# A store queued two heads later: the attention output's DMA behind the stack copies

## The chip, the cores and the metric

The kernel runs on one core of a Trainium2 chip. The metric is the time of one execution on the device in microseconds (us), and the kernel's time is the median over its runs. Beside the timed runs stands one profiled execution, whose trace gives the start and end of every instruction. A core has five instruction streams: TensorE (PE, with its weight loads shown as PEld), VectorE (DVE), ScalarE (ACT), GpSimd (POOL) and SyncE (SP). Here SP issues every DMA of the kernel, one after the other, in the order of its program: an instruction at the head of SP's queue that waits for data holds up all DMAs behind it.

## The reference, cut to what matters

```
x: 2048 tokens x 1024 channels, 32 heads of 32, 4 segments of 512 tokens
h = layernorm(x) * (1 + ca) + sa
q, k, v = h @ wq, h @ wk, h @ wv
for s in range(4):                                   # segments
    p = softmax(q_s k_s^T * scale + mask)            # causal, per head
    a_dot = p @ v_s
    a_mem = phi(q_s) M / (phi(q_s) z + 1e-6)
    o_s = g * a_mem + (1 - g) * a_dot                # g = sigmoid(beta), per head
    M += phi(k_s)^T v_s;  z += sum(phi(k_s))
x = x + ga * (o @ wo)
h = layernorm(x) * (1 + cb) + sb
x = x + gb * mixer(h)                                # two matrix products over the tokens, with GELU between
```

`sa`, `ca`, `ga`, `sb`, `cb`, `gb` come from `silu(c) @ w_mod`. The change touches only how `o` is carried to device memory between the attention and the product with `wo`.

## The kernel before, in words

The attention works in 32 iterations `t` (list `its`, line 313). One iteration is a group of four heads `g` and a segment `seg`: first all eight groups with segments 0 and 1, then all eight with segments 2 and 3. Within an iteration there are four heads `h`, so that there are 128 heads in all, numbered `n = 4 * t + h`. The loop at line 621 runs over `n` as a software pipeline. In step `n` it traces

- `scores` of head `n` (line 459): the product of queries and keys for the softmax, into PSUM; exponentials on ACT, the causal cut on POOL, and a split into two half-precision parts;
- `maxima` of head `n + 3` (LEADS, line 421): row maxima of that product. After each odd head the negated maxima of two heads are transposed into `nt`, and four small DMAs (line 445) put them into rows 96 and 97 of the stack tiles of the two heads, where `scores` reads them;
- `values` of head `n - 1` (VL, line 483): the product with the values. After the fourth head of an iteration four transposes put the iteration's output into PSUM (`ops`, line 510), ACT copies it to `ot` in SBUF (line 512; one buffer), and SP stores `ot` to the tensor `oT` in device memory (line 513);
- one piece of `project` for `n + 8` (LEADP, line 329): pieces 0 and 1 make keys and values, piece 2 transposes the keys, makes the queries, splits both into the tile `sg` (one buffer) and calls `stack` for heads 0 to 2, piece 3 calls `stack` for head 3;
- whatever `plan` has put down for step `n` in the table `todo`: weight prefetches, splits, stores of split weights.

`stack` (line 319) builds the operand tile `sk` of one head with three DMAs of 128 KB from `sg` (lines 325 to 327). There are eight such tiles, four for even and four for odd iterations.

So within step `4t + 4` the output of iteration `t` is finished and stored, and in step `4t + 6` the nt copies for heads 0 and 1 of iteration `t + 2` and the stacks of heads 0 to 2 of iteration `t + 3` are traced.

After the loop `out_proj` (line 688) reads `oT` in blocks of 128 tokens across all groups (`otr`, line 691) and multiplies with `wo` (line 706). Its blocks go in the order 0, 1, 8, 2, 9, and so on; blocks 0 to 7 lie in segments 0 and 1, blocks 8 to 11 in segment 2, which the last group stores in iteration 30, and 12 to 15 in segment 3, stored in iteration 31.

The order of instructions on each engine isn't the order of the text. A planner, asked for at line 997, goes through the traced instructions with a simulated timeline and puts each on its engine's queue when it is ready there; where several are ready, the one traced earlier goes first. `tc.issue_after(ins)` adds an edge: what is traced in its block on the engine of `ins` comes behind `ins` in that engine's queue. The edge orders the queue and is no wait for completion.

`marks` (line 448) holds, by head number and engine, an instruction behind which planned work may be put: V, A and G stand for DVE, ACT and POOL. The helper `behind(n, engines)` (line 451) opens such an edge for the mark of exactly that head, if there is one. The table `todo` and `plan` are defined at lines 592 to 595, and the loop takes a step's entries at line 642.

Of the kernel before, what the change touches and what calls it, by code (L numbers as in the profile page):

```python
# [7 lines left out]
F32 = mybir.dt.float32  # L8
# [9 lines left out]
S, D, H, DH, F = 2048, 1024, 32, 32, 3584  # L18
P = 128
NSEG, L = 4, 512  # L20
# [9 lines left out]
LEADP, LEADS, NSK = 8, 3, 8  # L30
XB = 4
VL = 1
# [8 lines left out]
LEADP = 8  # L41
LEADS = 3


def attention_and_mlp(ctx, tc, x, wq, wkv, wo, beta, w1, b1, w2, b2, c, wm_a, wm_b, out):
    nc = tc.nc
    V, A, G, T, SY = nc.vector, nc.scalar, nc.gpsimd, nc.tensor, nc.sync

    dram = ctx.enter_context(tc.tile_pool(name="dram", bufs=1, space=DRAM))
    oT = dram.tile([NG, P, S], F32, name="oT")  # L50
# [24 lines left out]
    def bank(tag, bufs, name):  # L75
        return psum.tile([P, 512], F32, tag=tag, bufs=bufs, name=name)
# [65 lines left out]
    def new_page(name):  # L142
        return page.tile([P, 2, 512], F32R, tag="page", bufs=16, name=name)
# [32 lines left out]
    def load_w(g, pr):  # L176
        res = W[pr, g] = {}
        for kind, part in (("v", 0), ("v", 1), ("q", 0)):
            load_part(g, pr, kind, part, res)
        if pr == 0:  # L180
            keep_w(g)
# [113 lines left out]
    b = late.__enter__()  # L295
# [12 lines left out]
    def reload_h(seg, ct):  # L308
        pg = new_page(f"h{seg}_{ct}")
        SY.dma_start(pg.bitcast(F32), hT1[seg - 2, ct])  # L310
        hpages[seg, ct] = pg
# [3 lines left out]
    st = {}  # L315

    last_sk = {}

    def stack(t, h):


        sk = st[t]["sk", h] = skt[t % 2][h]
        skf = sk.bitcast(F32)
        src = st[t]["sg"].bitcast(F32)[32 * h:32 * h + 32]
        SY.dma_start(skf[0:32], src[:, 0:3:2])
        SY.dma_start(skf[32:64], src[:, 0:4:3])
        last_sk[t, h] = SY.dma_start(skf[64:96], src[:, 1:3])

    def project(t, piece):
        pr, g, seg = its[t]  # L330
# [27 lines left out]
        elif piece == 2:  # L358
# [26 lines left out]
            for h in range(3):  # L385
                stack(t, h)
# [34 lines left out]
    def maxima(t, h):  # L421
        d = st[t]
        if h % 2 == 0:
            d["mx"] = b.tile([P, 2, 4], F32, tag="mx", bufs=2, name=f"mx{t}_{h}")
        mx = d["mx"]
        q, k = d["sk", h][0:96, 0], d["sk", h][0:96, 1]
        x = bank("s1", 2, f"sx_{t}_{h}")
        y = bank("s1", 2, f"sy_{t}_{h}")
        z = bank("s1", 2, f"sz_{t}_{h}")
        for i, o in ((0, x[:, 0:128]), (2, x[:, 128:512]), (1, y[:, 0:256]), (3, z)):  # L430
            T.matmul(o, q[:, 128 * i:128 * i + 128], k[:, 0:128 * i + 128], start=True, stop=True)  # L431
            marks[4 * t + h - LEADS, "V"] = V.tensor_tensor_reduce(  # L432
                o, o, mask[:, 384 - 128 * i:], 1.0, -3.0e38, op0=ALU.add, op1=ALU.max,
                accum_out=mx[:, h % 2, i:i + 1])
        if h % 2 == 0:
            return
        ps = bank("ms", 1, f"nmps{t}_{h}")
        T.transpose(ps[0:8, 0:128], mx.rearrange("p a b -> p (a b)"), ident)
        nt = [b.tile([8, P], F32R, tag=f"nt{i}", bufs=2, name=f"nt{i}_{t}_{h}") for i in range(2)]
        A.activation(nt[0], ps[0:8, 0:128], AF.Copy, scale=-1.0)  # L440
        V.scalar_tensor_tensor(nt[1], ps[0:8, 0:128], -1.0, nt[0].bitcast(F32), op0=ALU.mult, op1=ALU.subtract)
        for hh in range(2):
            sk = d["sk", h - 1 + hh]
            for part in range(2):
                SY.dma_start(sk[96 + part:97 + part, 0].bitcast(F32).rearrange("p (b n) -> p b n", n=128),
                             nt[part][4 * hh:4 * hh + 4].bitcast(F32))

    marks = {}

    @contextmanager  # L450
    def behind(n, engines):

        with ExitStack() as s:
            for e in engines:
                if (n, e) in marks:
                    s.enter_context(tc.issue_after(marks[n, e].ins))
            yield

    def scores(t, h):
# [23 lines left out]
    def values(t, h):  # L483
        pr, g, seg = its[t]
        d = st[t]
        am, ph = d["am"], d["ph", h]
        pv = bank("pv", 1, f"pv{t}_{h}").rearrange("p (a n) -> p a n", a=4)
        col = {0: lambda i: 128 * i, 1: lambda i: 512 + 128 * (i - 1), 2: lambda i: 1024 + 128 * (i - 2),
               3: lambda i: 896}
        n = 0  # L490
        for part, w in ((0, NV), (1, 65)):
            for i in range(4):
                for j in range(i + 1):
                    o = col[j](i)
                    T.matmul(pv[:, i, 0:w], ph[:, part, o:o + 128], d["vp"][:, j, h, 0:w], start=(n == 0),  # L495
                             stop=(n == 19), skip_group_check=True)
                    n += 1
        V.reciprocal(pv[:, :, 0], pv[:, :, 0])
        red = r_.tile([P, 4, 32], F32, tag="red", bufs=2, name=f"red{t}_{h}")
        V.tensor_reduce(red, pv[:, :, 1:97].rearrange("p a (c e) -> p a e c", c=3), axis=AX.X, op=ALU.add)  # L500
        ah = am[:, :, 32 * h:32 * h + 32]
        V.scalar_tensor_tensor(red if seg else ah, red, gate[:, 1, 4 * g + h:4 * g + h + 1],
                               pv[:, :, 0:1].to_broadcast([P, 4, 32]), op0=ALU.mult, op1=ALU.mult)
        if seg:
            G.tensor_tensor(ah, ah, red, op=ALU.add)
        if h < 3:
            return
        ps = bank("ms", 1, f"ops{t}")
        for i in range(4):
            T.transpose(ps[:, 128 * i:128 * i + 128], am[:, i], ident)  # L510
        ot = r_.tile([P, L], F32, tag="ot", bufs=1, name=f"ot{t}")
        A.copy(ot, ps)
        SY.dma_start(oT[g, :, L * seg:L * seg + L], ot)
        del st[t]

    mcol = const.tile([P, 4 * NK], F32, name="mcol")
# [6 lines left out]
    def mod_late(j, r):  # L523
        V.scalar_tensor_tensor(r, r, 1.0, scb, op0=ALU.mult, op1=ALU.mult, accum_out=mcol[:, j:j + 1])
        if j == 7:
            mod_rows(0, 8)
        if j == 31:
            V.tensor_scalar_add(mcol[:, 16:24], mcol[:, 16:24], 1.0)
            mod_rows(8, 32)

    def mod_rows(lo, hi):
        n = hi - lo
        ps = bank("ms", 1, f"mlt{lo}")
        T.transpose(ps[0:n, 0:128], mcol[:, lo:hi], ident)
        row = pj.tile([n, P], F32, tag="tmp", bufs=2, name=f"mrow{lo}")
        A.copy(row, ps[0:n, 0:128])
        SY.dma_start(modd.rearrange("a (b n) -> (a b) n", n=P)[lo:hi], row)

    def at(f, n):
        if 0 <= n < 4 * NI:  # L540
            f(n // 4, n % 4)
# [47 lines left out]
        for part, t in enumerate((hi, r)):  # L589
            SY.dma_start(wos[c2:c2 + 2, nh, :, part].rearrange("c p n -> p c n"), t)  # L590

    todo = {}

    def plan(n, f, engines=""):
        todo.setdefault(n, []).append((f, engines))

    def later(n, fetch, m, f, engines):

        got = []
        plan(n, lambda: got.append(fetch()))  # L600
        plan(m, lambda: f(got[0]), engines)
# [4 lines left out]
    for g in range(2, NG):  # L606
        n = 8 * g - 13
        plan(n, lambda g=g: W.__setitem__((0, g), {}))
        for kind, part, n0, n1 in (("v", 0, 0, 1), ("v", 1, 1, 3), ("q", 0, 2, 4)):
            later(n + n0, lambda g=g, kind=kind, part=part: fetch_part(g, kind, part),  # L610
                  n + n1, lambda r, g=g, kind=kind, part=part: split_part(g, kind, part, r), "A")
        plan(n + 4, lambda g=g: keep_w(g))
    for j in range(32):
        n = ML0 + MLS * j
        later(n, lambda j=j: mod_fetch(j), n + 2, lambda r, j=j: mod_late(j, r), "V")
    plan(WO0 - 3, lambda: spread(gaw, 0))
    for i in range(8):
        n = WO0 + WOS * i
        later(n, lambda i=i: wo_fetch(i), n + 2, lambda r, i=i: wo_split(i, r), "G")

    for n in range(-LEADS, 4 * NI + VL):
        at(scores, n)
        at(maxima, n + LEADS)
        at(values, n - VL)
        m = n + LEADP
        if 0 <= m + 4 < 4 * NI:
            t = (m + 4) // 4
            if its[t][:2] not in W:
                with tc.issue_after(last_sk[0, 3].ins):
                    load_w(its[t][1], its[t][0])  # L630
        if m >= 8:
            at(project, m)
        if 59 <= m < 67:
            seg, ct = 2 + (m - 59) // 4, 2 * ((m - 59) % 4)
            reload_h(seg, ct)
            reload_h(seg, ct + 1)
        if 4 * NI - 5 <= m < 4 * NI + 3:
            i = m - 4 * NI + 5
            for c in (2 * (i % 4), 2 * (i % 4) + 1):
                wop[c, i // 4] = new_page(f"wo{c}_{i // 4}")  # L640
                SY.dma_start(wop[c, i // 4].bitcast(F32), wos[c, i // 4])
        for f, engines in todo.pop(n, ()):
            with behind(n, engines):
                f()
    right.__exit__(None, None, None)
    for q in skp + [late, prj, paw]:
        q.__exit__(None, None, None)
# [227 lines left out]
    for u, (ph, g) in enumerate(units):  # L875
# [59 lines left out]
        t = tp.tile([P, 3, 512], F32, tag="tu", bufs=1, name=f"tu{g}")  # L935
# [65 lines left out]
```

## Time and profile before

| quantity | value |
|---|---|
| median of 3 runs | 2308.41 us |
| lowest and highest | 2302.83 and 2309.76 us |
| the profiled execution's own time | 2305.58 us |
| its span, first to last instruction | 2303.9 us |
| granted TensorE clock, mean | 0.983 of full |
| stores of `ot` (line 513) | 32, from 151.6 to 1075.0 us |
| stack copies, nt copies | 384 and 256 |

How rows of the profile are read. A row of a timeline has the start in us, the duration in us, the engine, the line of the kernel, the operation, output tile `<-` input tiles and a count; in brackets the idle time of the engine before it and what ended it. SPq is SP's queue of DMAs, and the duration there is that of issuing. A row of waits has who waited, for whom, the total in us, the number of times and the longest. A row of the chain of waits has start, duration and what the chain went through; "DMA" there is from issue to landing. In the rows by stretch, each engine has its busy time and, in brackets, its instructions.

### The profile page before, as it was taken

The page shows a single profiled execution, that of the slowest core. Times are in us where ns is not written, and L with a number is a line of the kernel's source. Part 1 is how long each engine was busy: PE and PEld are TensorE (multiplying, and loading weights), DVE is VectorE, ACT ScalarE, POOL GpSimd, SP SyncE. Part 2 cuts the span into 40 slices and gives each one's busy share as a digit, 9 for nine tenths or more (in the row PEclk, how much of TensorE's full clock was granted, in tenths as well). Part 3 has the DMA queues.
Part 4 walks back from the last instruction along what each step waited for, and adds up shares of the span by engine and source line. Part 5 has one row for each costly group of instructions (what it writes and reads, how often), then busy time and mean ns, then how long its engine had stood idle before and what let it go on. Part 6 is the DMA issues. An engine that isn't in the chain of part 4 may idle for free.

```text
span 2303.9 us, 38456 instructions
## 1 busy us (share of the span) xinstructions
PE 2232.7 (97%) x13866; PEld 1918.9 (83%) x13866; DVE 1703.9 (74%) x3814; ACT 1105.6 (48%) x2018; POOL 727.9 (32%) x835
## 2 busy tenths in 40 slices
PE   8989999998999999999999999999999999999999
PEld 7879888898998889977787888888887888888877
DVE  5666666775777777657988665688889787878787
ACT  5477766755656656654324333543334242424232
POOL 3165655655666767653001000023333000000000
PEclk9989999999999999989999999999999999999999
DMA  6656555677566566663466664556557441414133
GB/s 256 199 164 183 173 162 162 195 247 225 156 199 206 166 189 187 202 212 112 137 205 213 249 237 181 202 222 239 206 201 263 171 151 55 151 55 142 55 119 146
DMA packets 172593, 414.67 MB, mean 180 GB/s; under 512 B 17236, under 2 KB 71540, under 8 KB 163444
## 3 DMA queue, kind: packets, MB, share of 16 engines
q1 hardware_dynamic: 172404, 412.22, 54.7%
q8 instruction: 110, 1.80, 0.3%
q14 instruction: 79, 0.65, 0.1%
HBM read 236.23 MB, written 125.06 MB: 157 GB/s over the span
## 4 chain that ended last, share of the span: by engine, by line
PE 81%; DVE 9%; DMA 5%; ACT 2%; issue 1%; POOL 1%; SPq 0%; DVEq 0%; ACTq 0%
PE mx L798 41%; PE nps L193 14%; PE qps L201 7%; PE po L706 6%; PE pv L495 3%; DMA wr<-in_w_dram 1%; PE a L466 1%; PE sx L431 1%; DVE ac L805 1%; PE sz L431 1%; DVE bU L123 1%; PE rd L403 1%; DVE sp L123 1%; DMA sk<-nt 1%; PE a L469 1%
## 5 line engine op out<-in xcount | busy, mean ns | idle before, releaser
L798 PE MATMUL mx<-bU,sp 128*128 128x512 f32 x2352 | 537.0, 390 | 4.7 <-DVE ac L805 2.0
L798 PEld LDWEIGHTS mx<-bU,sp 128*128 128x128 f32 x2352 | 440.4, 188 | 100.8 <-DVE sp L123 2.7
L193 PE MATMUL nps<-wv,h 128*128 128x256 f32 x3072 | 438.2, 284 | 0.7 <-DVE sg L123 0.5
L798 PE MATMUL mx<-bA,sp 128*128 128x512 f32 x1764 | 432.0, 390 | 2.5 <-DVE sp L123 2.2
L120 ACT CAST sp<-wr 128x384 fp32r<-128x384 f32 (+2 forms) x408 | 217.1, 545 | 449.9 <-PE mx L798 379.6
L481 POOL TENSOR_TENSOR ph<-p,ph 128x640 f16<-128x640 f32 x256 | 379.6, 1504 | 159.0 <-ACT ph L479 153.5
L193 PEld LDWEIGHTS nps<-wv,h 128*128 128x128 f32 x3072 | 403.8, 190 | 6.8 <-DVE sg L123 0.7
L798 PEld LDWEIGHTS mx<-bA,sp 128*128 128x128 f32 x1764 | 330.5, 188 | 73.5 <-DVE sp L123 2.9
L123 DVE TENSOR_TENSOR sp<-wr,sp 128x384 fp32r<-128x384 f32 (+2 forms) x408 | 256.8, 641 | 29.4 <-ACT sp L120 29.2
L805 DVE TENSOR_TENSOR ac<-mx,ac 128x512 f32<-128x512 f32 x280 | 189.3, 685 | 91.2 <-PE mx L798 90.5
L201 PE MATMUL qps<-h,wq 128*128 128x512 f32 x768 | 200.7, 406 | 1.4 <-DVE r L356 1.4
L432 DVE CUSTOM_DVE_ANT_0 sx<-sx,mask 128x128 f32<-128x128 f32 (+1 forms) x256 | 109.5, 428 | 113.6 <-PE sx L431 111.9
L706 PE MATMUL po<-wo,ots 128*128 128x512 f32 x768 | 184.8, 400 | 5.3 <-DVE x L709 3.1
L479 ACT CAST ph<-p 128x1280 f16<-128x1280 f32 x128 | 160.8, 1257 | 41.1 <-POOL p L477 40.3
L706 PEld LDWEIGHTS po<-wo,ots 128*128 128x128 f32 x768 | 148.3, 194 | 38.0 <-issue 3.9
L201 PEld LDWEIGHTS qps<-h,wq 128*128 128x128 f32 x768 | 144.4, 194 | 30.2 <-DVE r L356 1.2
L798 PE MATMUL mx<-bB,sp 128*128 128x512 f32 x588 | 164.3, 389 | 0.0
L477 POOL TENSOR_SCALAR_AFFINE_SELECT p<-p 128x256 f32<-128x256 f32 x256 | 120.5, 480 | 129.2 <-ACT p L470 63.4
L495 PE MATMUL pv<-vp,ph 128*128 128x97 bf16 (+1 forms) x2560 | 146.6, 204 | 5.5 <-DVE mv L134 2.7
L495 PEld LDWEIGHTS <-ph 128*128 128x128 f16 x2560 | 117.5, 100 | 29.4 <-issue 12.1
L805 DVE TENSOR_TENSOR cc<-mx,cc 128x512 f32<-128x512 f32 x140 | 94.6, 683 | 49.9 <-PE mx L798 45.4
L798 PEld LDWEIGHTS mx<-bB,sp 128*128 128x128 f32 x588 | 110.4, 188 | 23.4 <-ACT bB L120 0.6
(173 smaller groups left out, 3206.0 us busy)
## 6 DMA issues: line engine op xcount, KB each, us to landing
sk<-sg SPq DMA_DIRECT2D x384, 128.0 KB
wr<-in_w_dram SPq DMA_DIRECT2D x28, 1024.0 KB
wr<-in_w_dram SPq DMA_DIRECT2D x32, 768.0 KB
bstu<-ucd SPq DMA_DIRECT2D x28, 768.0 KB
wsp<-wv SPq DMA_DIRECT2D x32, 512.0 KB
rawm<-in_wm_b_dram SPq DMA_DIRECT2D x32, 512.0 KB
wv<-wsp SPq DMA_DIRECT2D x32, 512.0 KB
pcd<-cc SPq DMA_DIRECT2D x14, 1024.0 KB
```

Source lines behind the costliest of these rows:

```text
L120: A.copy(hi, src)
L123: lo_eng.tensor_tensor(lo, src, hi.bitcast(F32), op=ALU.subtract)
L193: T.matmul(ps[:, aa], h[:, j, 128 * tt:128 * tt + 128], wt[:, i, o:o + 256], start=(n == 0), stop=(n >= 6 * NK - 2), skip_group_check=True)
L201: T.matmul(ps, wt[:, i, o:o + 128], h[:, j], start=(k + n == 0), stop=(3 * k + n == 3 * NK - 1))
L432: marks[4 * t + h - LEADS, "V"] = V.tensor_tensor_reduce(o, o, mask[:, 384 - 128 * i:], 1.0, -3.0e38, op0=ALU.add, op1=ALU.max, accum_out= ...
L477: G.affine_select(w, w, pattern=[[0, 2], [1, 128]], compare_op=ALU.is_ge, fill=0.0, base=0, channel_multiplier=-1)
L479: marks[n, "A"] = A.copy(ph[:, 0], p32)
L481: marks[n, "G"] = G.tensor_tensor(ph[:, 1, c], p32[:, c], ph[:, 0, c], op=ALU.subtract)
L495: T.matmul(pv[:, i, 0:w], ph[:, part, o:o + 128], d["vp"][:, j, h, 0:w], start=(n == 0), stop=(n == 19), skip_group_check=True)
L706: T.matmul(ps, os_[:, i, P * ct:P * ct + P], wop[ct, nh][:, j], start=(n == 0), stop=(n == 3 * NK - 1))
L798: T.matmul(ps, ops[q][:, i, P * k:P * k + P], b[:, j], start=(m == 0 and first), stop=(m == 3 * nk - 1), skip_group_check=True)
L805: V.tensor_tensor(d, ps, d, op=ALU.add)
```

## The change

The store of `ot` is no longer issued where `ot` has been copied, in step `4t + 4`. It is put down with `plan` for step `4t + 3 + VL + 2 = 4t + 6` with the engine letter "S", a new one for SP's queue.

The mark for "S" is set in two places: at the last copy of every stack, under the step in which that stack is traced (`max(h, 2)`, since heads 0 to 2 share a step), and at every nt copy. A later mark replaces an earlier one of the same step. In step `4t + 6` the nt copies come first and the stacks of iteration `t + 3` second, so that the mark is the last copy of its third stack; the store gets an edge behind that. `behind` now takes the newest mark among step `n` and the three before it. `marks` and `plan` are defined earlier in the text, and what is left in `todo` after the loop is traced there without an edge: the store of iteration 31, planned for step 130, since the loop ends with 128.

```diff
     last_sk = {}
+    marks = {}
...
-        last_sk[t, h] = SY.dma_start(skf[64:96], src[:, 1:3])
+        last_sk[t, h] = marks[4 * t + max(h, 2) - LEADP, "S"] = SY.dma_start(skf[64:96], src[:, 1:3])
...
-                SY.dma_start(sk[96 + part:97 + part, 0].bitcast(F32).rearrange("p (b n) -> p b n", n=128),
-                             nt[part][4 * hh:4 * hh + 4].bitcast(F32))
-
-    marks = {}
+                marks[4 * t + h - LEADS, "S"] = SY.dma_start(
+                    sk[96 + part:97 + part, 0].bitcast(F32).rearrange("p (b n) -> p b n", n=128),
+                    nt[part][4 * hh:4 * hh + 4].bitcast(F32))
...
-                if (n, e) in marks:
-                    s.enter_context(tc.issue_after(marks[n, e].ins))
+                m = next((i for i in range(n, n - 4, -1) if (i, e) in marks), None)
+                if m is not None:
+                    s.enter_context(tc.issue_after(marks[m, e].ins))
...
-        SY.dma_start(oT[g, :, L * seg:L * seg + L], ot)
+        plan(4 * t + 3 + VL + 2, lambda: SY.dma_start(oT[g, :, L * seg:L * seg + L], ot), "S")
...
+    for n in sorted(todo):
+        for f, _ in todo[n]:
+            f()
     right.__exit__(None, None, None)
```

`todo` and `plan` themselves are unchanged and only stand further up.

More of the change, by code (lines that the diff above doesn't have):

```diff
@@ L537, in mod_rows, with plan @@
         SY.dma_start(modd.rearrange("a (b n) -> (a b) n", n=P)[lo:hi], row)
+    todo = {}
+    def plan(n, f, engines=""):
+        todo.setdefault(n, []).append((f, engines))
     def at(f, n):
@@ L590, in wo_split @@
             SY.dma_start(wos[c2:c2 + 2, nh, :, part].rearrange("c p n -> p c n"), t)
-    todo = {}
-    def plan(n, f, engines=""):
-        todo.setdefault(n, []).append((f, engines))
     def later(n, fetch, m, f, engines):
```

## The prediction

> **What bounds the kernel now.** I read the page first, then busy time by stretch, then the waits of SP and of PE, then SP's own timeline around the stores, and last the end of the chain.
>
> The page:
>
> ```profile
> span 2303.9 us, 38456 instructions
> ...
> PE 2232.7 (97%) x13866; PEld 1918.9 (83%) x13866; DVE 1703.9 (74%) x3814; ACT 1105.6 (48%) x2018; POOL 727.9 (32%) x835
> ...
> PE 81%; DVE 9%; DMA 5%; ACT 2%; issue 1%; POOL 1%; SPq 0%; DVEq 0%; ACTq 0%
> ```
>
> TensorE sets the time: 97% of the span, 81% of the chain that ends last. A moved DMA can only be worth what TensorE waits because of DMAs. The stretches (columns: busy time of PE, PEld, DVE, ACT and POOL, granted clock, DMA share, GB/s) bound that for the attention, the only stage in which the store runs, and give the DMA load in two places used below:
>
> ```profile
> 100.00:990.00 890.00, 857.30 (x7463) 780.79 (x7463) 612.62 (x1861) 577.84 (x1059) 554.00 (x659) 0.97 0.63 184
> ...
> 516.00:526.00 10.00, 8.15 (x53) 6.96 (x52) 5.47 (x12) 5.01 (x8) 7.51 (x7) 0.88 0.90 313
> 776.00:788.00 12.00, 9.17 (x87) 8.38 (x86) 5.79 (x23) 5.42 (x12) 7.07 (x10) 0.93 0.70 199
> ```
>
> From 100 to 990 us PE is idle for 890.0 - 857.3 = 32.7 us in all, for every reason together. Next the two waits that name the argument: how long SP's queue stood at the store, and what TensorE waited for (100 to 1080 us):
>
> ```profile
> SPq L513 <- ACT ot L512: 98.5, 21, 12.7
> ```
>
> ```profile
> PE a L466 <- DMA sk<-nt: 8.2, 4, 2.8
> PE kps L363 <- DVE r L356: 7.4, 4, 4.1
> PE sz L431 <- DVE mx L432: 4.7, 5, 2.3
> ...
> PE sx L431 <- DMA sk<-sg: 1.5, 1, 1.5
> ```
>
> So the store blocks SP for 98.5 us in 21 places, which looks like much; but TensorE waits only 8.2 us (4 times) for the small copies of the negated maxima, and 1.5 us (once) for the stack copies. 9.7 us, 0.42% of the span, is all that SP's lateness shows on PE. The other rows are waits for DVE, which the store does not touch.
>
> **Was anything needed held behind the store?** The longest stall after the first ones, on SP and, beside it, on ACT:
>
> ```profile
> 841.65 2.62 SPq L445 DMA_DIRECT2D sk<-nt  x4
> 855.16 0.33 SPq L513 DMA_DIRECT2D oT<-ot  x1
> 855.59 0.37 SPq L520 DMA_DIRECT2D rawm<-in_wm_b_dram  x1
> 856.56 0.70 SPq L325 DMA_DIRECT2D sk<-sg  x1
> ...
> 866.20 0.59 SPq L327 DMA_DIRECT2D sk<-sg  x1
> ```
>
> ```profile
> 854.55 0.59 ACT L512 COPY ot<-ops 128x512 f32<-128x512 f32 x1 [3.19 <-PE ops L510]
> ...
> 855.95 0.59 ACT L120 CAST sg<-qps 128x512 fp32r<-128x512 f32 x1 [0.32 <-PE qps L201]
> ...
> 857.52 0.26 ACT L440 ACTIVATE nt<-nmps 8x128 fp32r<-8x128 f32 x1
> ```
>
> SP stands from 844.3 to 855.2 us at the store. What comes behind it is a prefetch (L520, used two heads later) and then the stack copies; but their source sg is written on ACT at 855.95, after ot, so the first stack copy starts 0.02 us after its data. The nt behind them is written at 857.52. The queue was blocked while nothing urgent was ready. I made the same comparison at all 32 stores: a stack or nt copy was ready ahead of the store and issued after it in only three places, near 333 us and 497 us, where TensorE waited for neither, and this one:
>
> ```profile
> 528.25 0.32 SPq L513 DMA_DIRECT2D oT<-ot  x1
> 529.55 0.33 SPq L520 DMA_DIRECT2D rawm<-in_wm_b_dram  x1
> ...
> 533.37 0.69 SPq L325 DMA_DIRECT2D sk<-sg  x1
> 535.45 0.65 SPq L326 DMA_DIRECT2D sk<-sg  x1
> 536.76 3.72 SPq L445 DMA_DIRECT2D sk<-nt  x4
> ```
>
> ```profile
> 544.69 0.50 PE L466 MATMUL a<-sk 98*128 98x512 f32 x1 [1.32 <-DMA sk<-nt]
> ```
>
> Here SP issues one DMA per 1.3 us, the store takes one of these slots, and TensorE then waits 1.32 us for nt. This is the one place where the old position costs TensorE anything.
>
> **The change part by part.**
>
> *Removed: the store at its old place.* Gain: one slot of 529.55 - 528.25 = 1.30 us at 528 us; elsewhere 0, covered because the data of what follows is later than ot. Bounds: 0 (TensorE's wait is filled by another DMA) to -8.2 us (all nt waits vanish). I take -1.3, since the other three nt waits have no store ahead of them.
>
> *Added: the store behind the third stack's last copy.* At 855 that is behind 866.20, 11 us later, where it waits for nothing: ot has long been written. SP issues the same number of DMAs; the store takes 0.33 us (tile view below). But there it joins a burst of twelve stack copies, and nt copies often follow. TensorE waited for nt right behind such a burst twice:
>
> ```profile
> 512.57 0.59 SPq L327 DMA_DIRECT2D sk<-sg  x1
> ...
> 517.61 2.63 SPq L445 DMA_DIRECT2D sk<-nt  x4
> ```
>
> ```profile
> 523.32 0.56 PE L466 MATMUL a<-sk 98*128 98x512 f32 x1 [1.85 <-DMA sk<-nt]
> ```
>
> ```profile
> 778.90 0.59 SPq L327 DMA_DIRECT2D sk<-sg  x1
> ...
> 781.22 2.63 SPq L445 DMA_DIRECT2D sk<-nt  x4
> ```
>
> ```profile
> 786.41 0.77 PE L466 MATMUL a<-sk 98*128 98x512 f32 x1 [2.83 <-DMA sk<-nt]
> ```
>
> A store ahead of these nt copies delays them by its issue, 0.33 us, plus its share of the transfer queues. Its size and the bounds of its landing:
>
> ```profile
> oT<-ot SPq DMA_DIRECT2D x32, 256.0 KB
> ```
>
> ```profile
> 1048.61 0.60 ACT ot L512
> ...
> 1049.23 2.34 DMA oT<-ot
> ...
> 1051.58 4.33 DMA otr<-oT
> ...
> 1057.04 9.84 PE po L706 x30
> ```
>
> Lower bound 0.33 us (bytes pass beside the copies), upper 0.33 + 2.34 = 2.67 us (nt lands only after the store). Between them I take its bytes at the rate that the queues moved in that stretch: 262 KB / 313 GB/s = 0.84 us, so 0.33 + 0.84 = 1.17 us; the stretch is at 0.90 DMA share, so nearer to shared bandwidth than to idle. Two places: +2.3 us (bounds +0.7 to +5.3).
>
> [...] Nothing measured here yet shows a small copy behind a store.
>
> *What the later store makes late.* ot has one buffer, so the next copy to ot waits for the store's landing:
>
> ```profile
> L513 SPq DMA_DIRECT2D oT<-ot x32: 319/326/1452, 151.6 to 1075.0; - x32
> ```
>
> (1075.0 - 151.6) / 31 = 29.8 us per group, 7.45 us per head. The store moves by about two heads, 15 us, and about as much is left before the next ot; the tightest is the group stored at 528 us, with its third stack and its next copy to ot here:
>
> ```profile
> 547.06 2.00 SPq L327 DMA_DIRECT2D sk<-sg  x1
> ```
>
> ```profile
> 556.25 0.59 ACT L512 COPY ot<-ops 128x512 f32<-128x512 f32 x1
> ```
>
> From 549.06 to the copy are 7.2 us, against 2.34 for landing. Covered; with that cover gone ACT would stand, at worst, some 2 us per group. The last stores have no stack behind which to go: group 29 goes behind an nt copy of its step, group 30 behind an nt copy two heads earlier, group 31 after the loop without a mark. In SP's queue nothing lies between their old and new steps, so they stay where they are: 0 us. This matters since group 30's store is on the chain: it lands at 1051.57, the load of oT waits for it, and PE goes on at 1057.04.
>
> *Other edits.* The search of up to three heads back in the helper changes no older use, since each of those finds its own head's mark: 0. Moving the plan's definition costs 0.
>
> *Sum:* -1.3 + 2.3 = +1.0 us. The profiled execution took 2305.58 us with its span of 2303.9; so 2306.6 for such an execution. The runs' median is 2308.41, 2.8 above it, and the runs lie between 2302.83 and 2309.76; I set the forecast on the median: 2309.4, called 2309.5.
>
> **The rivals.**
>
> *Slower, nt behind the store's bytes.* Place: nt copies issued within 5 us behind the third stack, where TensorE's margin is under 5 us; I count four of the nine such groups (near 451, 518, 552, 781 us). Price: 4 x 2.67 = 10.7 us, 2319. It decides from the point at which a store's landing holds nt for more than some 2 us. For: 0.90 DMA share at 516 to 526. Against: 0.70 at 776. [...]
>
> *Faster, another order.* The build orders every engine's instructions by a simulated timeline, so a moved DMA can shift copies, and with them PE's order, all through the attention. PE's 32.7 us idle is the stock: a third of it less, with the nt waits (8.2) among it, is 11 us: 2298. For: many waits are under 2 us and hang on the order. Against: neither TensorE's work nor its buffers change; the same reshuffle can lose as much.
>
> *Slower, the end.* If group 30's store is really issued two heads later, 14.9 us, the load of oT and PE's next output projection follow: 2308.4 + 14.9 = 2323. Against: no copy stands between.
>
> *The change doesn't do what it says.* If the mark isn't found, the store stays in the queue where ot is ready: 2308.4. Against: each group up to 28 has a third stack in that very step.
>
> **How the numbers follow.** Forecast 0.48; mark without effect 0.06; faster order 0.20; nt behind the store 0.21; late end 0.05. A measurement of this kernel can tell about 0.3%, 6.9 us, from no change. So same 0.54, faster 0.20, slower 0.26. The likeliest case's own range is 2302 to 2315 (0 to +8 us of unknown costs on runs that spread by 3 us either way). For 8 in 10 it is widened to 2297 (the other order and the runs' spread) and 2321 (the nt rival).
>
> **What would show it.** Right: SP's wait for ot at the store, 98.5 us, falls below 10; the store comes right behind a third stack's last copy; TensorE's wait for nt stays between 5 and 14 us; PE idle from 100 to 990 near 33 us. The nt rival: TensorE's nt wait above 15 us, with a store just ahead. Another order: PE idle moves by 8 us or more in rows that name DVE or ACT. The end: the last two stores further behind their ot copies than now. The forecast is wrong if the time moves by more than 0.3% either way.

## The result, and the profile after

| | before | after |
|---|---|---|
| median of 10 runs each | 2305.68 us | 2312.99 us |
| lowest and highest | 2300.37 and 2310.79 us | 2307.56 and 2315.30 us |
| ratio, with its 95% interval | | 1.0026 (1.0015 to 1.0037) |
| span of the profiled execution | 2303.9 us | 2311.9 us |

The forecast was 2309.5 us with no change beyond 0.3% as the likeliest case. The changed kernel is 0.26% slower: 0.0026 x 2305.68 = 6.0 us (3.5 to 8.5). (The ratio on record is not the quotient of the two medians, which is 1.0032; the ratios below aren't either.) That lies within the 0.3%, but its interval excludes "no change", and it is six times the +1.0 us of the prediction's sum. So the case that was named came, and the sum behind it was too small.

The page of the changed kernel:

```profile
span 2311.9 us, 38437 instructions
...
PE 2233.2 (97%) x13866; PEld 1922.2 (83%) x13866; DVE 1704.8 (74%) x3814; ACT 1108.6 (48%) x2018; POOL 729.0 (32%) x835
...
PE 77%; DVE 8%; DMA 8%; ACT 3%; issue 2%; POOL 2%; SPq 1%; DVEq 0%; ACTq 0%; POOLq 0%
```

TensorE's busy time is the same (2232.7 us before, 2233.2 after). Of the 8.0 us of span 7.5 are idle time of TensorE, and in the chain that ends last the DMAs' share rises from 5% to 8%. By stretch, first after and then before (columns: busy time of PE, PEld, DVE, ACT and POOL, granted clock, DMA share, GB/s):

```profile
100.00:990.00 890.00, 853.86 (x7395) 777.97 (x7394) 610.49 (x1854) 578.06 (x1054) 550.17 (x652) 0.97 0.62 184
990.00:1080.00 90.00, 78.99 (x560) 64.00 (x559) 56.66 (x159) 47.38 (x76) 53.39 (x63) 0.87 0.54 171
```

```profile
990.00:1080.00 90.00, 82.22 (x525) 66.74 (x524) 61.95 (x159) 45.25 (x73) 46.97 (x54) 0.87 0.55 182
```

In the attention PE is idle for 890.0 - 853.86 = 36.1 us against 32.7 before, and in the 90 us around the attention's end for 11.0 us against 7.8. The two make 6.7 of the 8.0 us. This sets one execution against one other; e9 below shows how far two of the same order differ.

SP's wait at the store, and TensorE's waits from 100 to 1080 us, both after:

```profile
SPq L514 <- ACT ot L513: 11.2, 2, 9.7
```

```profile
PE a L467 <- DMA sk<-nt: 6.8, 6, 3.0
PE sx L432 <- DMA sk<-sg: 6.0, 3, 4.1
PE sx L432 <- DVE mx L433: 6.0, 9, 1.4
PE sy L432 <- DVE mx L433: 4.9, 7, 2.2
PE pv L496 <- DVE red L503: 4.7, 3, 1.9
```

The stall of SP fell from 98.5 us in 21 places to 11.2 in 2, and TensorE got nothing for it. SP stands elsewhere instead: its wait for ACT to write nt grew from 42.3 to 68.3 us. TensorE's nt wait fell only from 8.2 to 6.8 us, and the wait for stack copies rose from 1.5 to 6.0. Added up by what was waited for, over all rows from 100 to 1080 us, the waits for DMAs went from 9.7 to 12.8 us, for DVE from 22.9 to 25.7, for POOL from 1.3 to 3.6. The store stands where the change puts it, here inside the burst, with nt 5 us behind it, and TensorE waits for that nt 3.03 us (1.85 before):

```profile
512.50 0.59 SPq L328 DMA_DIRECT2D sk<-sg  x1
513.14 0.58 SPq L514 DMA_DIRECT2D oT<-ot  x1
513.82 0.61 SPq L326 DMA_DIRECT2D sk<-sg  x1
...
518.45 2.63 SPq L446 DMA_DIRECT2D sk<-nt  x4
```

```profile
414.79 0.45 PE L432 MATMUL sx<-sk 96*128 96x128 f32 x1 [4.14 <-DMA sk<-sg]
...
522.56 0.56 PE L467 MATMUL a<-sk 98*128 98x512 f32 x1 [3.03 <-DMA sk<-nt]
```

The move also changed the planner's order. The instruction lists of the two kernels differ on PE in 6186 of 13610 positions, on DVE in 1043 of 3262, and among SP's other DMAs in 361 of 1206. Two theories follow. PLACE: the store costs by standing among the stack copies, ahead of nt. ORDER: the place is harmless, and the other order on the engines costs the 6 us.

### The profile page after: what moved, and what is told of

The parts are those of the page before. It is cut to its first block, busy times and chain, and to the rows that moved or that the text cites. A ratio compares the mean times of both kernels' runs of the same rounds, so it can differ in the third digit from the quotient of the medians.

```text
span 2311.9 us, 38437 instructions
## 1 busy us (share of the span) xinstructions
PE 2233.2 (97%) x13866; PEld 1922.2 (83%) x13866; DVE 1704.8 (74%) x3814; ACT 1108.6 (48%) x2018; POOL 729.0 (32%) x835
## 4 chain that ended last, share of the span: by engine, by line
PE 77%; DVE 8%; DMA 8%; ACT 3%; issue 2%; POOL 2%; SPq 1%; DVEq 0%; ACTq 0%; POOLq 0%
PE mx L802 40%; PE nps L193 12%; PE qps L201 7%; PE po L710 5%; PE pv L496 3%; DMA xb<-x1d 1%; PE sx L432 1%; PE a L467 1%; DMA x1e<-xb 1%; PE sz L432 1%; DVE st L128 1%; POOL ph L482 1%; DMA wr<-in_w_dram 1%; DMA sk<-nt 1%; PE a L470 1%
## 5 line engine op out<-in xcount | busy, mean ns | idle before, releaser
L710 PEld LDWEIGHTS po<-wo,ots 128*128 128x128 f32 x768 | 145.7, 191 | 37.3 <-issue 3.9
L496 PE MATMUL pv<-vp,ph 128*128 128x97 bf16 (+1 forms) x2560 | 151.4, 205 | 8.3 <-DVE red L503 4.7
```

Of the source, the lines that this page charges most:

```text
L710: T.matmul(ps, os_[:, i, P * ct:P * ct + P], wop[ct, nh][:, j], start=(n == 0), stop=(n == 3 * NK - 1))
```

## The experiments

To tell order from place, the order of each engine was held by edges, which order a queue and wait for nothing. In the kernels below that are built so, only the list of SP's DMAs differs:

```diff
+    for e in engines:
...
+        o = [traced[e][k] for k in np.arange(len(d)) + d]
...
+        for a, b in zip(o, o[1:]):
+            tc.add_manual_dep(b, a.name, mybir.DependencyInfo(mybir.DependencyClass.NoSync, mybir.DependencyReason.DATA),
+                              reason="pin")
...
+        pin(tc, nc, ['PE', 'DVE', 'Activation', 'Pool', 'SP'])
```

Each ratio is to runs of before taken beside it. "Order" is that of the compute engines and of SP's other DMAs.

| run | engines' order | the store | ratio to before, 95% |
|---|---|---|---|
| e1_move_only | before | new place | 1.0030 (1.0018 to 1.0042) |
| e2_order_only | after | old place | 1.0092 (1.0073 to 1.0111) |
| e3_store_twice | before | new place, and a second store behind it | 1.0050 (1.0031 to 1.0068) |
| e4_one_head | before, by the planner | planned one head later; stays where it was | 1.0000 (0.9987 to 1.0014) |
| e5_extra_store | before | old place, 256 KB copy at the new | 1.0029 (1.0014 to 1.0044) |
| e6_extra_tiny | before | old place, 2 KB copy at the new | 1.0033 (1.0020 to 1.0045) |
| e7_six_home | before | 6 old, the others new | 1.0010 (0.9997 to 1.0024) |
| e8_order_harmless | after | first slot of SP with ot ready | 1.0029 (1.0014 to 1.0043) |
| e9_pinned_before | before | old place | 1.0006 (0.9993 to 1.0019) |
| e10_behind_nt | before | 19 behind the next nt copies | 0.9997 (0.9983 to 1.0012) |
| e11_three_heads | its own | behind the fourth stack | 1.0046 (1.0028 to 1.0064) |
| e12_only_one | before | 1 new, 31 old | 1.0001 (0.9987 to 1.0014) |

**e1_move_only and e2_order_only: one half of the change each.** The first has before's order and the stores at their new place, the second after's order and each store behind the DMA that it had ahead of it before.

> The store stands where the changed kernel has it in SP's queue; the order of all instructions on TensorE, VectorE, ScalarE and GpSimd, and of SP's other DMAs, is held to that of the kernel before. Theory ORDER (the 0.26% comes from the planner's other order on the engines, not from the store): 1.000 of before within 0.0012, TensorE's idle time 58 to 61 us as before (58.7). Rival PLACE (the store's 256 KB behind the stack copies delay the nt and later stack copies): 1.0026 of before or more, TensorE idle 64 to 68 us, its waits for nt and sg copies 3 us or more above before's 9.7.

> The reverse: every engine and SP's other DMAs in the order of the changed kernel, the stores back behind the DMAs that they follow in the kernel before, so that SP waits for ot again (about 100 us in all). Theory ORDER: 1.0026 of before within 0.0015, TensorE idle 64 to 69 us. Rival PLACE: 1.000 of before within 0.0012, TensorE idle near 59 us.

Measured: 2315.15 us for the place alone, 2328.65 for the order alone. ORDER falls by e1: with no instruction of PE, DVE, ACT or POOL in another position, the place costs 0.30% (0.0030 x 2306.65 = 6.9 us, 4.2 to 9.7). Its trace adds little to its times:

```profile
PE a L466 <- DMA sk<-nt: 13.1, 6, 3.6
```

With 1.5 us for stack copies that is 14.6 us against 9.7 in before, more than the 3 us that PLACE asked for; but TensorE's idle time from 100 to 1080 us is 42.9 us against 40.5, less than the 5 us more that it asked for. And the profiled execution took 2309.3 us, 5.9 less than e1's median, while e9 below, with nothing moved, reads 14.3 and 43.7 us. So where e1 loses its time can't be read from this trace. The second was meant as the other half and is worse than both kernels. Its waits:

```profile
SPq L513 <- ACT ot L512: 87.4, 18, 12.3
```

```profile
PE a L466 <- DMA sk<-nt: 16.7, 11, 4.0
PE sx L431 <- DMA sk<-sg: 7.6, 4, 4.2
```

In after's order the old position is not harmless: SP stands 87.4 us at the store, nearly as long as before (98.5), but here TensorE's waits for nt and for stack copies make 24.3 us, against 12.8 in after, which has the same order. So the length of the stall alone doesn't set the loss. That it is what stands behind the store is argued, not shown. e2 measures an order together with a place of the store that doesn't suit it.

**e3_store_twice: the suspected cost doubled.** e1 with a second 256 KB store of `ot`, to a spare tensor.

```diff
         SY.dma_start(oT[g, :, L * seg:L * seg + L], ot)
+        SY.dma_start(oT2[g, :, L * seg:L * seg + L], ot)
```

> As the move alone with the order held, but each store is issued twice in a row, the second into a spare tensor, so that the suspected cost (issue and bytes ahead of the nt copies) doubles. Theory ORDER: at most 0.1% above the move alone (32 more issues of 0.33 us, of which only those ahead of an nt copy that TensorE waits for count). Rival PLACE: 1.005 of before, twice the loss, TensorE's wait for nt copies above 12 us.

Measured: 2316.88 us, 1.0050 against 1.0030 for one store. The intervals overlap, so a second store costs more or nothing; this run doesn't decide. TensorE's wait for nt is above the 12 us that PLACE asked for, 15.2, but in an execution of 2325.2 us, 8.3 above the median.

**e4_one_head: the store planned one head later instead of two.**

```diff
-        plan(4 * t + 3 + VL + 2, lambda: SY.dma_start(oT[g, :, L * seg:L * seg + L], ot), "S")
+        plan(4 * t + 3 + VL + 1, lambda: SY.dma_start(oT[g, :, L * seg:L * seg + L], ot), "S")
```

> The store planned one head later instead of two, by the planner as in the changed kernel. It then stands behind the nt copies of the step before, and the planner's order on the four compute engines comes out the same as in the kernel before. Theory ORDER: 1.000 of before within 0.0012, though SP's wait for ot shrinks. Rival PLACE: between 1.000 and 1.0026. A third theory, that SP's stall at the store costs TensorE something: faster than before, 0.998 or less.

Measured: 2306.66 us, 1.0000. The planner's order on the four compute engines is that of before, and SP stands at the store as ever, though a shorter wait was expected:

```profile
SPq L514 <- ACT ot L513: 101.1, 22, 12.4
```

In SP's queue only three of the 32 stores stand one DMA later than in before, and all else is in before's order. So this plan left the store practically where it was. The run is not half of the change but a control: edges, marks and plan by themselves cost nothing that can be told.

**e5_extra_store and e6_extra_tiny: the place without the move.** Before's order with the stores at home; at the new place a copy of `ot` to a spare tensor is added, of 256 KB in the first and of one row, 2 KB, in the second. It adds transfers and leaves nothing out.

```diff
         SY.dma_start(oT[g, :, L * seg:L * seg + L], ot)
+        SY.dma_start(oT2[g, 0:1, L * seg:L * seg + L], ot[0:1])
```

> The kernel before with its order held and its stores where they were, and one more copy of ot (256 KB, into a spare tensor) issued behind the last copy of the third stack of the iteration three later, where the changed kernel has the store. SP's wait for ot stays. Theory BYTES (256 KB in the burst delay the nt copies behind them, and TensorE's longer wait lowers its clock): as much as the move alone, 1.002 to 1.0045. Rival FREED (the move costs because SP, no longer held at the store, issues prefetches and stacks at other times): 1.000 within 0.0013, since SP is held as before.

> The same with only one row of ot in the extra copy (2 KB): SP's issue slot alone. Theory BYTES: 1.000 within 0.0013. Rival SLOT (one more issue of 0.6 us ahead of the copies that TensorE waits for): 1.002 or more.

Measured: 1.0029 and 1.0033. TensorE's wait for nt (from 100 to 1080 us), first with 256 KB and then with 2 KB:

```profile
PE a L467 <- DMA sk<-nt: 16.7, 6, 3.9
```

```profile
PE a L467 <- DMA sk<-nt: 17.2, 7, 4.5
```

Traces with no DMA added there read 8.2 to 12.0 (before, e4, e9, e10). A DMA at this place costs about the same whether it is the store (e1, 1.0030), a copy beside the store at home (1.0029) or a 128th of its bytes (1.0033), so BYTES falls. FREED falls too: SP is held at the store as in before (104.4 us in e5 and 99.8 in e6, 98.5 in before), and the cost is there. So it isn't the bytes ahead of nt that cost, but one more DMA in the burst. A copy added elsewhere in the queue wasn't tried, so these two runs alone don't exclude that any added DMA costs; against it stands e1, which adds none.

**e7_six_home: where it costs.** e1 with the stores of iterations 8, 11, 12, 17, 20 and 26 in their old place, those behind which the trace of e1 fell back against before's.

> The move alone with the order held, but six of the 29 stores (iterations 8, 11, 12, 17, 20 and 26, those whose new place stands ahead of an nt copy that TensorE waited for, near 428, 521, 555, 700, 784 and 964 us) stay at the old place; 23 are moved. Theory BYTES: most of the loss is gone, 1.000 to 1.001, TensorE's wait for nt 8 to 10 us. If the loss is spread over all moved stores: 1.002 to 1.003.

Measured: 1.0010, which lies between none and e1, and its interval reaches both 0.9997 and 1.0024. By the middle of the interval the six carry two thirds of the loss, and the run excludes neither that they carry all of it nor that they carry a fifth (0.06 of 0.30%). TensorE's wait for nt, expected at 8 to 10 us, was 13.2.

**e8_order_harmless: after's order with the store out of the burst.** Each store stands in the first slot of SP after `ot` is written in the trace of after.

> Every engine and SP's other DMAs in the order of the changed kernel, and each store in the first slot of SP's queue after its ot is ready in that kernel's trace, so that it neither holds SP nor joins the stack burst. It shows the planner's other order by itself. If the order is neutral: 1.000 within 0.0015 of before. If it costs (it holds a wait of 4.1 us for a stack copy at 411 us that before hasn't): 1.0015 to 1.003. If it gains and the place takes it back: 0.998.

Measured: 1.0029. This would be the price of the order, if the store were harmless there, but the trace (of an execution of 2303.0 us, 10.7 below the run's median) shows SP still standing at it, and the wait of 4.1 us for a stack copy that after has near 411 us is here as well (4.56 us; in e2 one of 4.2), with no store in that burst:

```profile
SPq L513 <- ACT ot L512: 63.9, 23, 12.2
```

```profile
407.40 0.45 PE L431 MATMUL sx<-sk 96*128 96x128 f32 x1 [4.56 <-DMA sk<-sg]
```

That wait belongs to the order. How much of the 0.29% is order and how much is SP's 63.9 us, this run leaves open.

**e9_pinned_before: the control.** Before's order, held by edges, with nothing moved.

> The kernel of before with every engine's order held by edges to the order that it has anyway: nothing is moved. PLACE (what e1, e5 and e6 lost hangs on what stands in SP's queue behind the third stack): 0.999 to 1.0015 of before, TensorE's waits for nt 7 to 10 us, its own idle time near before's 58.7 us. EDGES (holding the order by edges is itself what costs 0.3%, so that e1, e5, e6 and e8 measured the edges): 1.002 to 1.004, with the waits of e1 and e8 but no store in the bursts.

Measured: 1.0006, so the edges cost nothing that can be told. Its profile is worth more than its time. The program's order is that of before, instruction for instruction, and yet the profiled span is 2308.5 us against 2303.9, and the waits (from 100 to 1080 us) and two of their places read:

```profile
PE a L466 <- DMA sk<-nt: 12.0, 6, 4.3
...
PE sx L431 <- DMA sk<-sg: 2.3, 2, 1.5
```

```profile
431.79 0.77 PE L466 MATMUL a<-sk 98*128 98x512 f32 x1 [3.24 <-DMA sk<-nt]
...
789.58 0.77 PE L466 MATMUL a<-sk 98*128 98x512 f32 x1 [4.28 <-DMA sk<-nt]
```

Before's trace has no such wait at the first place and 2.83 us at the second. Two executions of the same order thus differ by 4.6 us of span and by 3.8 us of nt wait; the 12.0 us are above the 7 to 10 that were expected of it. TensorE's idle time from 100 to 990 us is 35.7 us here and the DMAs' share of the chain 10%, so the 36.1 us and the 8% of the changed kernel's trace above say nothing of the change. A difference of that size between two single traces shows nothing, and a stall at one of these places in e1 or after isn't the store's doing.

**e10_behind_nt: as late, but behind nt.** Before's order; 19 stores stand behind the next nt copies, where `ot`'s next copy leaves room, and 13 at home.

> Before's order on all engines; 19 stores stand late, but behind the next nt copies instead of ahead of them, where ot's next copy leaves room for it; the other 13 stand in their old place. PLACE AHEAD OF NT (the store costs because the nt copies and the first copies behind the burst come one slot later): 0.999 to 1.0015 of before, TensorE's waits for nt at most 10 us. LATENESS OR FULL QUEUE (any store taken out of the stretch in which SP stands idle and put among the stack copies or prefetches costs): 1.002 to 1.004, as e1, with waits for sg or split operands if not for nt.

Measured: 0.9997, an interval that doesn't touch e1's. SP's wait at the store and TensorE's for nt:

```profile
SPq L513 <- ACT ot L512: 26.8, 6, 10.2
```

```profile
PE a L466 <- DMA sk<-nt: 10.3, 6, 2.4
```

Most of the stall is gone here too, and those 19 stores are later than in the changed kernel; it neither costs nor gains. The time doesn't even show that ACT, in two places, now waits for the store before it writes `ot` again (from the view of the stores, who waited for them):

```profile
  ACT ot L512: 10.1, 2
```

For these 19 stores being late is free. That being in the burst is what costs fits this and e6, but the comparison with e1 isn't clean: of the 29 stores that e1 puts into bursts, ten are at home here, and four of them (iterations 11, 12, 17 and 26) are among the six of e7. Spread evenly over 29 stores, e1's 0.30% would leave 0.20% for 19 of them (an estimate), which lies above e10's interval; if most of it lies at those four, e10 says little. The same 19 stores inside the bursts weren't tried.

**e11_three_heads: another order of the planner.** The changed kernel with `VL + 3`, which puts the store behind the fourth stack.

```diff
-        plan(4 * t + 3 + VL + 2, lambda: SY.dma_start(oT[g, :, L * seg:L * seg + L], ot), "S")
+        plan(4 * t + 3 + VL + 3, lambda: SY.dma_start(oT[g, :, L * seg:L * seg + L], ot), "S")
```

> The changed kernel with the store planned one head later still (4t + 3 + VL + 3), behind the fourth stack's last copy; the planner's order is free and differs from both others (PE in 5739 positions from before, in 6414 from after). PLACE with a neutral order: 0.999 to 1.002 of before, since fewer nt copies follow the fourth stack, nt waits below 10 us. ORDER (each new order of the planner costs or gains a few us by itself): anything from 0.996 to 1.006, and PE's idle time differs from before's 58.7 us in rows that name DVE and ACT, by more than the nt waits differ.

Measured: 2318.56 us, 1.0046, the slowest of the three positions that the planner was given (one, two and three heads: 1.0000, 1.0026, 1.0046; the first left the store where it was, and the intervals of the other two overlap). SP waits for `ot` at the store once, 9.6 us, in iteration 30. TensorE's waits from 100 to 1090 us:

```profile
PE a L467 <- DMA sk<-nt: 7.9, 7, 2.2
PE kps L364 <- DVE r L357: 6.7, 6, 3.7
PE pv L496 <- DVE red L503: 5.2, 4, 2.2
PE sx L432 <- DVE mx L433: 3.9, 8, 1.3
PE po L710 <- DMA wo<-wos: 3.7, 1, 3.7
PE qps L201 <- DVE r L357: 3.6, 3, 2.2
```

The nt wait is no longer than before's. What is longer stands in rows that the store doesn't touch: pv for red 5.2 us (0.7 in before), qps 3.6 (1.4). That speaks for the order, as far as one trace can; the same place in before's order wasn't tried.

**e12_only_one: one store moved.** Eight traces with before's order had one place where all four with a DMA added to the burst differed from the three that had none there and no store ahead of it moved into a burst (before, e9, e10). It is behind the store of iteration 17. In before and in e1 the two executions run alike up to 700 us, and then SP's queue reads, before first:

```profile
690.40 0.59 SPq L327 DMA_DIRECT2D sk<-sg  x1
691.09 1.60 SPq L168 DMA_DIRECT2D wv<-wsp  x1
...
696.93 2.64 SPq L445 DMA_DIRECT2D sk<-nt  x4
```

```profile
688.70 0.58 SPq L513 DMA_DIRECT2D oT<-ot  x1
...
690.67 0.60 SPq L327 DMA_DIRECT2D sk<-sg  x1
691.38 1.30 SPq L168 DMA_DIRECT2D wv<-wsp  x1
...
696.93 2.63 SPq L445 DMA_DIRECT2D sk<-nt  x4
```

nt is issued at the same instant, 696.93 us, and lands later (at 702.40 us in before's chain of waits and at 703.77 in e1's): TensorE waits 2.21 us in before and 3.57 in e1 (and 1.69 in e9, where nothing is moved, 4.46 in e6 with its 2 KB). In the order before, e9, e1, e6:

```profile
702.54 0.47 PE L466 MATMUL a<-sk 98*128 98x512 f32 x1 [2.21 <-DMA sk<-nt]
```

```profile
704.30 0.47 PE L466 MATMUL a<-sk 98*128 98x512 f32 x1 [1.69 <-DMA sk<-nt]
```

```profile
703.91 0.77 PE L466 MATMUL a<-sk 98*128 98x512 f32 x1 [3.57 <-DMA sk<-nt]
```

```profile
705.82 0.76 PE L467 MATMUL a<-sk 98*128 98x512 f32 x1 [4.46 <-DMA sk<-nt]
```

Behind the wait the granted clock reads 1.00 in before and 0.50 in e1, in this order:

```profile
704.00:708.00 4.00, 4.00 (x20) 3.29 (x18) 1.51 (x3) 0.73 (x2) 0.87 (x2) 1.00 0.37 109
```

```profile
704.00:708.00 4.00, 4.00 (x15) 3.01 (x16) 1.70 (x4) 1.68 (x3) 0.41 (x1) 0.50 0.02 6
```

A wait that is 1.4 us longer (3.57 against 2.21) goes with half clock at this place. The same matmuls (those that start from 690.03 to 723.00 us in before) take 33.0, 32.5 and 32.4 us in before, e9 and e10, but 37.3, 37.5, 36.2 and 37.6 in e1, e3, e5 and e6: +4.6 us between the means. Worked from the starts of these matmuls in each trace, that would be two thirds of the loss at one place. So this store alone was moved.

> Before's order on all engines, and of the 32 stores only that of iteration 17 (at 675.6 us in before) is moved, behind the third stack, near 688.7 us. ONE SITE (the one place where all executions with a DMA added to the burst differ from those without: TensorE's wait for nt near 703 us is 3.6 to 4.5 us against 1.6 to 2.2, and half clock follows, 36.2 to 37.6 us against 32.4 to 33.0 for the same matmuls): the wait is 3.3 us or more, the stretch from 690 to 723 us takes 36 us or more, and the time is 1.0010 to 1.0030 of before (+4.3 us is 1.0019). SPREAD (the loss is made up of small pieces at many stores, and this site differs because the stores ahead of it were moved too): the wait stays at 1.6 to 2.2 us, and the time is 0.9990 to 1.0010.

Measured: 2306.92 us, 1.0001 (0.9987 to 1.0014). The place did nearly what was expected, the time did not:

```profile
702.06 0.76 PE L466 MATMUL a<-sk 98*128 98x512 f32 x1 [3.06 <-DMA sk<-nt]
```

```profile
704.00:708.00 4.00, 4.00 (x12) 3.12 (x11) 1.50 (x3) 0.54 (x2) 0.86 (x2) 0.58 0.02 5
```

The wait is 3.06 us (expected 3.3 or more), a clock of 0.58 is there, and the stretch takes 36.3 us; the ratio excludes +4.3 us (1.0019) all the same. Either this stretch is as long in some of before's runs too, or the 3 to 4 us are given back elsewhere. For the first speak two traces. In e7 this store was at home, the wait was 2.18 us, and the clock fell to 0.50 nonetheless, from 708 to 712 us (35.9 us for the stretch). And e4, which was not among the eight, has the store at home (675.31 us) and nothing added to any burst, and reads:

```profile
701.95 0.76 PE L467 MATMUL a<-sk 98*128 98x512 f32 x1 [2.05 <-DMA sk<-nt]
```

```profile
704.00:708.00 4.00, 4.00 (x10) 3.08 (x10) 1.51 (x3) 0.43 (x1) 0.85 (x2) 0.50 0.03 10
```

The same matmuls take 35.7 us in it, at a ratio of 1.0000. So at this place the longer wait belongs to the DMA in the burst (1.6 to 2.2 us in the five traces without one there, 3.1 to 4.5 in the five with one), while half clock and the longer stretch come without it as well (0.50 and 35.7 us in e4). ONE SITE falls as the account of the time. The 0.30% needs more than this store, and where it lies among the 29 stays open.

## Why the prediction was right, and where its sum was not

**TensorE bounds, and SP's stall holds nothing urgent: right.** The stall of 98.5 us went and nothing was gained. e10 shows it in before's order (26.8 us left, 0.9997). e4 can't show the other side, since it left the store in its place. The 11.2 us that are left exceed the "below 10" because the last two stores, which don't move, still wait for their `ot`. The -1.3 us for the slot at 528 us can't be seen: TensorE's wait there, 1.32 us, is shorter than what two executions of the same order differ by.

**The store joins the burst, two places, +2.3 us: the direction right, the size not.** This is the term that failed. e1 is the move without another order, so it holds this term and the slot that was counted at -1.3 us: together +1.0 us in the prediction, and 6.9 us (4.2 to 9.7) measured. The term's upper bound, +5.3 with nothing gained at the slot, reaches only the lower part of that interval. That the cost comes by later copies is borne out by the traces in before's order: TensorE's waits for nt and stack copies from 100 to 1080 us make 9.7, 12.0, 12.2, 12.3 and 14.3 us in before, e4, e12, e10 and e9, with at most one DMA added to a burst, and 14.6, 16.3, 18.4, 19.7 and 20.1 in e1, e7, e3, e6 and e5, with 23 or more. Between 14.3 and 14.6 this separates nothing; the others stand apart.

What was wrong in the term are its places and its price. At the place near 518 us e1's wait for nt is 1.81 us against 1.85 in before; at the one near 781 us it is 3.59, shorter than the 4.28 of e9, where nothing was moved. The place of e12 wasn't on the list since its nt copies come 6 us behind the burst. The price by bytes: 2 KB cost as much as 256 KB (1.0033 and 1.0029), so neither 0.84 us for the bytes nor the store's landing of 2.34 us was the thing to add. And the wait was priced as itself, without the clock of 0.50 that stands behind it at the place of e12 in e1; how much of the 6.9 us that is, the runs don't show, since in e4 the clock fell to 0.50 there without any DMA added.

**The slower rival, nt behind the store's bytes: its place right, its reason not.** It priced four places at 2.67 us, 10.7 us in all, and the measured loss lies between it and the forecast. But its mechanism was the bytes, which e6 refutes: 2 KB cost 1.0033, 256 KB 1.0029. That nt lands later behind a store does show at the place of e12, at 703.77 us in e1 against 702.40 in before with the same issue time. What the runs don't bear out is a price that scales with the bytes ahead.

**Another order: taken as neutral, which no run supports.** The rival's mark was idle time that moves by 8 us in rows naming DVE or ACT; after shows 2.8 us more for DVE, so the mark was not reached. The 0.26 for a slower time held nothing for it. But of the four kernels with an order other than before's (after, e2, e8, e11) none is below 1.0026, so "the same reshuffle can lose as much" wasn't a reason to count it at nothing. Yet place and order don't add: place alone 0.30%, after's order with the store in another place 0.29% or 0.92%, both together 0.26%. after's order was planned around the store in its new place, and may suit that place; no run shows it. How the 0.26% divides is open.

**One buffer of `ot`, and the last stores: right.** ACT's longest waits don't name the store in after, and the last two stores stand directly behind their copies (the third last, forecast to stay, stands 5.1 us behind its own). The rival of the late end didn't come.

**The arithmetic against one execution.** A sum of +1.0 us, built on waits of 1 to 3 us, was set against traces that differ by 4.6 us in span for the same order. It could not be better than its bounds, and these left the order out. That the result fell inside the 0.3% was owed to a bound wider than the sum, not to the sum.

## What to carry to other kernels

A long stall of a queue isn't worth its length: here SP's stall at the store fell from 98.5 to 26.8 us in e10, and the time stayed (0.9997). Look at what becomes ready behind it before removing it. A DMA that nobody waits for is best tried behind the copies that somebody does wait for, not in the burst ahead of them: here 19 stores behind them cost nothing, 29 in the bursts cost 0.30%, and a DMA of 2 KB in the burst (1.0033) was no cheaper than one of 256 KB (1.0029). Before a wait is put down to a change, profile the unchanged program a second time, and see how far the profiled execution lies from the median of the runs: here a second profile alone moved single waits by 3 us.

## What was unexpected of the hardware

One DMA of 2 KB added per group, 29 of them right behind the third stack's copies, cost 1.0033 (1.0020 to 1.0045), as much as 256 KB each (1.0029). At the place of e12 it goes with a later landing of the small copies, not a later issue: in before and in e1 they are issued at 696.93 us and land at 702.40 and 703.77. By which step of the transfer the delay comes, no run here shows.

The clock's answer to a wait isn't settled by the wait's length here. A wait of 2.21 us before the matmul at 702.54 us leaves the clock at 1.00; one of 2.18 us at the same matmul in e7 is followed by 0.50:

```profile
706.78 0.76 PE L466 MATMUL a<-sk 98*128 98x512 f32 x1 [2.18 <-DMA sk<-nt]
```

```profile
708.00:712.00 4.00, 4.00 (x14) 3.15 (x12) 1.78 (x5) 1.26 (x3) 0.86 (x2) 0.50 0.05 20
```

What does settle it, no run here shows.
